# Both MLP halves in block pairs, one block turned on TensorE, and the order from a list scheduler

## The chip, the cores and the metric

The kernel runs on one core of a Trainium2 chip. The metric is the device time of one execution in microseconds. TensorE (PE) multiplies into eight banks of accumulators; VectorE (DVE) and ScalarE (ACT) do the element-wise work; GpSimd (POOL) and SyncE (SP) mostly issue DMAs here. Each engine works off its own instructions in the order in which the program emits them, and they wait for one another by semaphores.

## The reference

```python
x = A_x                       # 2048 rows x 640
xn = _layernorm(x, axis=-1)
# Fourier half: real part of a DFT along the hidden axis and along the sequence
a = einsum("bsd,ed->bse", xn, dft_hid_re); b = einsum("bsd,ed->bse", xn, dft_hid_im)
y = einsum("ts,bse->bte", dft_seq_re, a) - einsum("ts,bse->bte", dft_seq_im, b)
# MLP half: 640 -> 1536 -> 640
h = gelu(einsum("bsd,df->bsf", xn, w1) + b1)
return x + y + einsum("bsf,fd->bsd", h, w2) + b2
```

All is in 32-bit floats. The kernel writes each operand as a high half rounded to TensorE's format (ACT, a copy) and a low half, the rest (DVE, a subtraction), and makes one product of 128x128 weights with 512 columns out of three matmuls: high x high, high x low, low x high.

## The kernel before, in words

The MLP half comes first. The 2048 rows are four blocks of 512; the 640 inputs are five chunks of 128, the 1536 hidden columns twelve units `f` of 128, the 640 outputs five chunks. Layer one of a unit costs five products (15 matmuls, `hidden`, L308, the matmul at L320), layer two five more (`output`, L363, whose three matmuls are at L300 to L302 in `product`). Each unit goes through `gelu` (L354): ACT takes the bias and the gelu out of the bank, ACT writes the high half (`high`, L185), DVE the low half (`low`, L188).

Block 0 comes plain: its rows are normalized, turned on TensorE (`transpose_x`, L680, 20 turns of 128x128), split, and multiplied unit by unit while W1 and W2 are loaded and split. Blocks 1 and 2 go together in `pair` (L1039), six steps `k` of two units each. With sums and differences of the blocks' chunks (the forms `ua`, `va`, `vb`, `t1` to `t4`, `oa`, `ob`) and of W1's columns (the pieces A to D, `make_pieces`, L891), four units of layer one (two units, two blocks) take 18 products where four plain ones take 20. A step holds them in seven windows over three banks; copies out of banks and additions of two banks on ACT and DVE join them. The forms of blocks 1 and 2 are made by turning 32x32 tiles on DVE, after the rows went through memory (`put_z`, `make_forms`). The units of block 2 go to memory (`keep`, L930, issued by POOL) and come back later (`load_unit`), since only one block's five layer-two sums fit beside a pair. Block 3 comes plain again, with W1 loaded and split once more; W2 stays on chip in high and low halves. Block 1's, 2's and 0's results take the bias on ACT, are turned on DVE, added to the residual rows and stored (`finish`, `turn_sum`, `store_sums`).

Beside this run preparations for the Fourier half: five chunks of the hidden DFT matrices are loaded, turned, combined and split (`load_w`, `turn_w`, `prep_w`), and the normalized rows are combined into `xab` and `xc` (`build`, L596). The Fourier half follows from `es_rows.close()` on, and takes the larger part of the time. Before all stand 19 warm-up matmuls (L666).

The order of everything around the matmuls in the MLP half is written out by hand: `background`, `late`, `beside_pair`, `between` and `fourier_step` say what is emitted beside which unit or window.

Of the kernel before, what the change touches and what calls it, by code (L numbers as in the profile page):

```python
# [10 lines left out]
F32 = mybir.dt.float32  # L11
# [4 lines left out]
P = 128  # L16
# [10 lines left out]
def kernel(  # L27
# [71 lines left out]
    gs = dram.tile([NF, P, TB], F32, name="gs")  # L99
# [16 lines left out]
    def bank(k):  # L116
# [3 lines left out]
    pool("pad", side="right").tile([P, 120], F32, name="padr")  # L120
# [4 lines left out]
    MV = const.tile([P, 4, 6], F32, name="mv")  # L125
# [14 lines left out]
    PLACES = [  # L140
# [9 lines left out]
    ]  # L150
    slots = {}
# [5 lines left out]
    def open_place(tag, size, keys):  # L157
        t = place(tag, (P, size // 4))
        for k, key in enumerate(keys):
            slots[key] = t[:, k * 2 * D : (k + 1) * 2 * D].rearrange("p (a b) -> p a b", a=2)  # L160
# [30 lines left out]
    def weave(*lists):  # L191

        for row in zip_longest(*lists):
            for f in row:
                if f:
                    f()
# [5 lines left out]
    xt, slot = {}, {}  # L202

    def load_x(c, eng=nc.sync, k=None, home=None):

        slot[c] = c % NC if k is None else k
        xt[c] = (row_places if home is None else home)[:, slot[c]]
        eng.dma_start(xt[c], x[c * P : (c + 1) * P])

    def ln_stats(c):  # L210
        m = MV
        st = ST[c % 2]
        half = D // 2
        for h in range(2):
            nc.vector.bn_stats(st[:, h, :], xt[c][:, h * half : (h + 1) * half])
        nc.vector.bn_aggr(m[:, slot[c], 0:2], st.rearrange("p a b -> p (a b)"))

    def ln_scale(n):

        m = MV[:, :n]  # L220
        ve, r, t = m[:, :, 2], m[:, :, 3], m[:, :, 4]
# [3 lines left out]
        nc.vector.scalar_tensor_tensor(t, r, -0.5, r, op0=ALU.mult, op1=ALU.mult)  # L225
        nc.vector.tensor_tensor(t, t, ve, op=ALU.mult)
        nc.vector.scalar_tensor_tensor(r, t, 1.5, r, op0=ALU.add, op1=ALU.mult)

    def ln_apply(c, eng=nc.vector):
        m = MV[:, slot[c]]  # L230
        eng.tensor_scalar(xt[c], xt[c], m[:, 0:1], m[:, 3:4], op0=ALU.subtract, op1=ALU.mult)

    def ln_apply_chunked(dst, c, j0=0, j1=ND):

        m = MV[:, slot[c]]
# [8 lines left out]


    XT, zt = {}, {}
    Z = {}

    def new_xt(t):
        w = mr.tile([P, ND, 2, TB], F32R, tag="xt", bufs=1, name=f"xt{t}")  # L250
        for j in range(ND):
            XT[j] = w[:, j]
# [4 lines left out]
    def transpose_z(key, z, j):  # L257
        zt[key] = mr.tile([P, TB], F32, tag="zt", bufs=2, name=f"zt{key}")
        nc.vector.transpose(zt[key].rearrange("p (n i) -> p n i", i=B), z[:, :, j * B : (j + 1) * B])

    def prep_xt(key, j):
        split(XT[j][:, 0], XT[j][:, 1], zt.pop(key))

    W1, W2, w1r, w2r = {}, {}, {}, {}


    AGAIN = (0, 1, 2, 3, 8, 9, 10, 11, 6, 7, 4, 5)

    def load_w1(i, eng=nc.sync):

        if i >= 3 * NF:
            return
        f0 = (i % NF if i < 2 * NF else AGAIN[i - 2 * NF]) * P
        t = early.tile([P, ND, P], F32, tag="w2r" if i == NF + 5 else "w1r", bufs=3, name=f"w1r{i}")
        w1r[i] = t
        v = w1.rearrange("(q c i) f -> q i c f", q=Q, i=B)
        for q in range(Q):
            eng.dma_start(t[q * B : (q + 1) * B], v[q, :, :, f0 : f0 + P])

    def load_w2(i, eng=nc.sync):  # L280
        if i >= NF:
            return
        t = early.tile([P, D], F32, tag="w2r", bufs=3, name=f"w2r{i}")
        w2r[i] = t
        eng.dma_start(t, w2[i * P : (i + 1) * P, :])

    def prep_w1(i, n=None):
        if i < NF:
            W1[i] = slots[1, i]
            split(W1[i][:, 0], W1[i][:, 1], w1r.pop(i if n is None else n).rearrange("p a b -> p (a b)"))  # L290

    def prep_w2(i):
        if i < NF:
            W2[i] = slots[2, i]
            split(W2[i][:, 0], W2[i][:, 1], w2r.pop(i), perm=True)
# [7 lines left out]


    NG = NT * NF
    HT, oacc, xo = {}, {}, {}

    def hidden(g, part=slice(None)):  # L308
        i = g % NF
        acc = bank((5 if g < NF else 0) + g % 3)  # L310
        kinds = ((0, 0), (0, 1), (1, 0))
        steps = [(j, k) for j in range(ND) for k in range(3)]
        if g == 0:
            steps = FIRST
        if g == 1:

            steps.sort(key=lambda s: s[1] == 2)
        for n, (j, k) in list(enumerate(steps))[part]:
            a, b = kinds[k]
            nc.tensor.matmul(  # L320
                acc, W1[i][:, a, j * P : (j + 1) * P], XT[j][:, b], start=n == 0, stop=n == len(steps) - 1
            )
        return acc

    def term(g, acc, a=None):

        if a is None:
            a = mr.tile([P, TB], F32, tag="ab", bufs=2, name=f"ab{g}")
        nc.scalar.activation(a, acc, AF.Copy)
        return a  # L330

    def unit(g, acc, plus=None, a=None):

        i = g % NF
        if a is None:
            a = mr.tile([P, TB], F32, tag="ab", bufs=2, name=f"ab{g}")
        if plus is not None:
            add(a, plus, acc)
            acc = a
        nc.scalar.activation(a, acc, AF.Gelu_apprx_tanh, bias=b1c[:, i : i + 1])  # L340
        return a

    def split_unit(g, a, fill=lambda k: None):
        hs = mr.tile([P, 2, TB], F32R, tag="hs", bufs=3, name=f"hs{g}")
        HT[g] = hs
        high(hs[:, 0], a)
        fill(1)
        low(hs[:, 1], a, hs[:, 0])


    FIRST = [(0, 0), (0, 2), (1, 0), (1, 2), (0, 1), (2, 0), (2, 2), (1, 1), (3, 0), (3, 2)]
    FIRST += [(2, 1), (4, 0), (4, 2), (3, 1), (4, 1)]

    def gelu(g, acc, fill=lambda k: None):  # L354

        a = unit(g, acc)
        fill(0)
        split_unit(g, a, fill)


    OBANKS = ((0, 1, 2, 3, 4), (0, 1, 2, 3, 4), (5, 6, 7, 3, 4), (3, 4, 5, 6, 7))

    def output(g, es=range(ND)):  # L363
# [308 lines left out]

    for p in PLACES[:7]:
        open_place(*p)
# [1109 lines left out]
```

## Time and profile before

| | us |
|---|---|
| median of two runs (850.91 and 851.31) | 851.11 |
| span of the profiled execution | 848.5 |
| its MLP half, to the first matmul of the Fourier half | 329.8 |
| TensorE busy | 842.5 |
| DVE busy | 687.1 |
| ACT busy | 368.8 |

A row of the groups by line reads: line, engine, operation, what is written and read, shapes, count, then busy time, mean nanoseconds of one, and the engine's idle time before them with what ended it. Matmuls overlap, so the mean of one is longer than their spacing. A row of the chain of waits reads: start, duration, what ran. The windows give each engine's busy time within a stretch.

### The profile page before, as it was taken

Reading aid. Unit: us, or ns where it says so; the run is one execution under the profiler, and the core shown is the slowest. Engines: PE = TensorE matmul, PEld = TensorE weight load, DVE = VectorE, ACT = ScalarE, POOL = GpSimd, SP = SyncE. Lnnn points to the kernel's source line nnn. Section 1 sums busy time; section 2 is a strip of 40 time slices with the busy share of each in tenths; the row PEclk is TensorE's granted clock in tenths of the full one; section 3 lists DMA queues with packets and bytes.
Section 4 is the critical chain, followed back from the end, with each engine's and each line's share of the span. In section 5 each row is a group of like instructions: output and inputs, shape, how many; then the busy total and the mean of one; then the engine's idle time right before and its main releaser. Section 6 shows DMA issues by size and latency. Waiting matters only on the chain.

```text
span 848.5 us, 10660 instructions
## 1 busy us (share of the span) xinstructions
PE 842.5 (99%) x3741; PEld 698.6 (82%) x3741; DVE 687.1 (81%) x912; ACT 368.8 (43%) x527; POOL 67.6 (8%) x116
## 2 busy tenths in 40 slices
PE   9999999999999999999999999999999999999998
PEld 7888888888888888888888888888888888888887
DVE  7969888767854778979979787899977998886687
ACT  7655666545453555443444343232322433223241
POOL 0440024222301000000000000000000000000002
PEclk9999999999999999999999999999999999999999
DMA  7995757878987897948744679663744799805354
GB/s 222 291 247 163 149 159 249 265 222 298 254 203 201 336 321 139 208 118 198 156 137 107 167 219 292 158 142 95 218 151 156 230 234 230 311 19 180 124 168 112
DMA packets 197094, 166.53 MB, mean 196 GB/s; under 512 B 59601, under 2 KB 168145, under 8 KB 196529
## 3 DMA queue, kind: packets, MB, share of 16 engines
q1 hardware_dynamic: 187296, 140.42, 61.8%
q0 software_dynamic: 7600, 24.91, 8.8%
q10 hardware_dynamic: 2144, 0.52, 0.3%
q8 instruction: 29, 0.48, 0.2%
q14 instruction: 25, 0.20, 0.1%
HBM read 115.75 MB, written 46.14 MB: 191 GB/s over the span
## 4 chain that ended last, share of the span: by engine, by line
PE 99%; DVE 0%; issue 0%
PE banks L301 30%; PE banks L300 30%; PE banks L302 30%; PE banks L320 10%; PE banks L666 1%; PE banks L682 0%; DVE zeros L655 0%; DVE yo L1706 0%; DVE warm L657 0%
## 5 line engine op out<-in xcount | busy, mean ns | idle before, releaser
L301 PE MATMUL banks<-as,xab 128*128 128x512 f32 (+1 forms) x417 | 160.1, 384 | 0.0
L300 PE MATMUL banks<-as,xab 128*128 128x512 f32 (+1 forms) x417 | 160.1, 384 | 0.0
L302 PE MATMUL banks<-as,xab 128*128 128x512 f32 (+1 forms) x417 | 160.1, 384 | 0.0
L186 ACT ACTIVATE as<-r 128x1024 fp32r<-128x1024 f32 x80 | 85.0, 1062 | 171.2 <-PE banks L302 147.4
L189 DVE TENSOR_TENSOR as<-r,as 128x1024 fp32r<-128x1024 f32 x80 | 97.1, 1215 | 38.1 <-ACT as L186 38.0
L301 PEld LDWEIGHTS banks<-as,xab 128*128 128x128 f32 x417 | 78.3, 188 | 15.6
L300 PEld LDWEIGHTS banks<-as,xab 128*128 128x128 f32 x417 | 78.3, 188 | 15.5
L302 PEld LDWEIGHTS banks<-as,xab 128*128 128x128 f32 x417 | 78.3, 188 | 15.4
L301 PE MATMUL banks<-as,xc 128*128 128x512 f32 x224 | 87.1, 389 | 0.0
L300 PE MATMUL banks<-as,xc 128*128 128x512 f32 x224 | 87.1, 389 | 0.0
L302 PE MATMUL banks<-as,xc 128*128 128x512 f32 x224 | 87.1, 389 | 0.0
L186 ACT ACTIVATE as<-rt 128x1024 fp32r<-128x1024 f32 x32 | 34.0, 1062 | 72.5 <-PE banks L302 57.9
L320 PE MATMUL banks<-xt,xab 128*128 128x512 f32 x240 | 56.8, 390 | 0.0
L189 DVE TENSOR_TENSOR hs<-ab,hs 128x512 fp32r<-128x512 f32 x36 | 24.7, 685 | 36.2 <-ACT hs L186 36.2
L320 PEld LDWEIGHTS banks<-xt,xab 128*128 128x128 f32 x240 | 45.0, 188 | 9.4
L301 PEld LDWEIGHTS banks<-as,xc 128*128 128x128 f32 x224 | 42.0, 188 | 8.8
L302 PEld LDWEIGHTS banks<-as,xc 128*128 128x128 f32 x224 | 42.0, 188 | 8.7
L300 PEld LDWEIGHTS banks<-as,xc 128*128 128x128 f32 x224 | 42.0, 188 | 8.7
L1280 POOL DMA_DIRECT2D out_dram<-u x4 | 2.6, 657 | 568.3 <-DVE u L463 568.3
L300 PE MATMUL banks<-hs,xc 128*128 128x512 f32 x120 | 46.7, 389 | 0.0
L301 PE MATMUL banks<-hs,xc 128*128 128x512 f32 x120 | 46.7, 389 | 0.0
L302 PE MATMUL banks<-hs,xc 128*128 128x512 f32 x120 | 46.7, 389 | 0.0
(240 smaller groups left out, 1679.8 us busy)
## 6 DMA issues: line engine op xcount, KB each, us to landing
raw<-in_A_dft_seq_re_dram SPq DMA_DIRECT2D x64, 256.0 KB, 5.4
raw<-in_A_dft_seq_im_dram SPq DMA_DIRECT2D x64, 256.0 KB, 5.1
w1r<-in_B_w_dram SPq DMA_DIRECT2D x144, 80.0 KB, 3.3
wit<-wst POOLq DMA_DIRECT2D x15, 384.0 KB, 4.3
wit<-wst POOLq DMA_DIRECT2D x20, 256.0 KB, 4.2
forms_ab<-xab SPq DMA_DIRECT2D x4, 1280.0 KB, 7.6
xab<-wit SPq DMA_DIRECT2D x13, 384.0 KB, 4.1
row<-xn SPq DMA_DIRECT2D x14, 320.0 KB, 5.3
```

Source lines behind the costliest of these rows:

```text
L186: nc.scalar.activation(h, s, AF.Copy)
L189: nc.vector.tensor_tensor(l, s, h.bitcast(F32), op=ALU.subtract)
L300: nc.tensor.matmul(acc, wh, mh, start=first, stop=False, skip_group_check=goes_on)
L301: nc.tensor.matmul(acc, wh, ml, start=False, stop=False, skip_group_check=goes_on)
L302: nc.tensor.matmul(acc, wl, mh, start=False, stop=last, skip_group_check=goes_on)
L320: nc.tensor.matmul(acc, W1[i][:, a, j * P : (j + 1) * P], XT[j][:, b], start=n == 0, stop=n == len(steps) - 1)
L666: nc.tensor.matmul(wacc, warm[:, :P], warm, start=True, stop=True)
L1280: queues[q % len(queues)].dma_start(rows_of(out, t)[:, rows, q * DQ + c0 : q * DQ + c1], src[q * B : (q + 1) * B])
```

## The change

The MLP half is written anew; the Fourier half keeps its code, but for two places that exchange names.

- Layer one: blocks 0 and 1 are one pair, blocks 2 and 3 another, each with six steps of 18 products (seven windows of two or three products). Plain blocks are gone.
- Pair 0 begins with block 0 alone: for each even unit, the two windows that need no form of block 1 are run first (`first_unit`, `a_units`, `a_rest`), the unit goes on to layer two, and the sum of the first window is kept on chip (`U[k]`). The other 13 products follow in `rest_of_pair`, after ACT has written `U[k]` back to a bank. In pair 1 the sum goes from one bank to another instead.
- Block 1 is normalized and turned on TensorE like block 0, into banks 0 to 4; its forms are made from there. Blocks 2 and 3 are normalized, written to memory, read back and turned on DVE.
- W1's columns are loaded once for block 0's first windows (the even units) and once for each pair. W2 is split once and stays, in other places than before, in the order 0, 2, ..., 10, 1, 3, ..., 11.
- The units of blocks 1, 2 and 3 all go to memory (`gs` grows to four blocks) and come back for layer two, which runs for block 0 beside pair 0 and for the others one after another.
- Normalizing of blocks 1 to 3 uses ACT for most rows.
- Two of the five chunks of the hidden matrices are prepared after the forms of pair 0 (`w_early`), three after those of pair 1 (`w_late`).
- The order of emission comes from a list scheduler that runs while the program is built: each piece of work is a generator that yields an engine, an assumed duration, a function and its needs; `work` keeps an assumed clock for each engine and always emits the step with the least start time plus weight. 93 weights stand in the source.

The diff, cut to its core:

```diff
-    gs = dram.tile([NF, P, TB], F32, name="gs")
+    gs = dram.tile([NT, NF, P, TB], F32, name="gs")
...
+    LAG = {"pe": 0.3, "act": 0.12, "dve": 0.12}
...
+    def pe(n, fn, *needs, w=None):
+        return op("pe", n * 0.68, fn, needs, w)
+    def act(n, fn, *needs, w=None, table=None):
+        return op("act", 0.1 + n * 0.00094, fn, needs, w) + (table,)
+    def dve(n, fn, *needs, w=None):
+        return op("dve", 0.08 + n * 0.00108, fn, needs, w)
...
+    def work(goal=None):
+        while threads and (goal is None or goal not in done):
...
+                start = max(t, clock[want[0]])
+                score = start + (th[2] if want[4] is None else want[4])
+                if best is None or score < best[0]:
+                    best = score, start, th
...
+    def a_units():
+        mark(("va", 0), 14.9)
+        for k in range(1, 6):
+            n, t = yield BANK
+            t = yield pe(2, lambda: window(bank(n), f"Au{k % 2}", 0, "ua", True), ("A", k), t)
+            spawn(a_rest(k, n, t), W("a_rest", 0.0))
...
+    def a_rest(k, n, t):
+        acc = bank(n)
+        t = yield act(TB, lambda: copy(U[k], acc), t, w=W("op1", -0.3))
+        mark(("U", k), t)
+        t = yield pe(3, lambda: window(acc, f"Av{k % 2}", 0, "va", False, (f"Av{k % 2}", 2, "oa0")), t)
...
+    def next_rows():
...
+            t = yield pe(0.7, lambda: [turn_row(c, j) for c in range(NC)], *needs)
+            mark(("T", j), t)
...
+    def rest_of_pair(p, k, nx, nz, t):
...
+        tx = yield pe(2, lambda: window(x_, c, 0, "t2", False), (p, "x", k), (p, "C", k), ("X", p, "t20"), ("X", p, "t21"))
...
+        tv = yield act(TB, lambda: copy(v, x_), tx, tv, w=W(f"op3{p}", -0.3))
+        tz = yield pe(3, lambda: window(z_, d, 2, "t1", True, (b, 2, "ob0")),
+                      t, (p, "D", k), (p, "B", k), ("X", p, "t10"), ("X", p, "t11"), ("X", p, "ob0"))
...
+        tc = yield act(TB, lambda: copy(zc, z_), tz, tc, w=W(f"op2{p}", -0.3))
+        tx = yield pe(2, lambda: window(x_, d, 0, "t3", False), tv, ("X", p, "t30"), ("X", p, "t31"))
...
+        spawn(z_and_b(p, k, z_, nz, tc, v, tv), W(f"z_and_b{p}", -0.01))
+        ta = yield dve(TB, lambda: add(zc, zc, x_), tx, tc, w=W(f"op4{p}", -0.3))
...
+        tx = yield pe(3, lambda: window(x_, b, 0, "t4", False, (b, 2, "oa0")), ta, ("X", p, "t40"), ("X", p, "t41"))
...
+    def first_pair():
+        yield ("X", 0, "t10")
+        for k in range(NF // 2):
+            nx, t = yield BANK
+            t = yield act(TB, lambda: copy(bank(nx), U[k]), t, ("U", k))
...
+            spawn(rest_of_pair(0, k, nx, nz, t), W(f"rest0{k // 5}", 0.001))
+            yield (0, "t3", k)
...
+    def second_pair():
...
+            t = yield pe(2, lambda: window(bank(ny), f"Bu{k % 2}", 0, "ua", True), t, (1, "Au", k))
...
+            t = yield act(TB, lambda: copy(bank(nx), bank(ny)), t, tx, w=W("op5", -0.3))
+            mark((1, "x", k), t)
+            spawn(other_unit(k, ny, t), W(f"other{k // 5}", 0.002))
...
+            spawn(rest_of_pair(1, k, nx, nz, tz), W(f"rest1{k // 5}", 0.001))
...
+    def rows_again():
...
+        for token in (("rest", 0), (0, "z1", 5), *((0, "x", k) for k in range(2, 6))):
+            yield token
+        Z[2] = region("wa", "z2", F32).rearrange("p (n d) -> p n d", d=DQ)
+        t = yield dma(6.1, lambda: load_z(Z[2], 2), ("xn", 2), n=4)
```

More of the change, by code (lines that the diff above doesn't have):

```diff
@@ L302, in product @@
         nc.tensor.matmul(acc, wl, mh, start=False, stop=last, skip_group_check=goes_on)
[L305 to L323, printed above, removed]
@@ L651 @@
+    yt2 = rows.tile([P, 2, TB], F32, name="yt2")
+    zeros = yt2[:, 0]
+    warms = [early.tile([P, D], F32R, tag=f"raw{k}", bufs=1, name=f"warm{k}")[:, :TB] for k in range(3)]
     for c in range(NC):
@@ new lines, with halves @@
+    first_unit(slice(1, None))
+    clock.update(pe=14.8, act=13.2, dve=13.9, sp=13.5, pool=5.0, dma=14.0)
+    for c in range(NC, 2 * NC):
+        mark(("x", c), 12.0 + 0.5 * (c - NC))
+    RAW = Slots()
+    RAWA = Slots()
+    XT = Slots()
+    TMP = Slots(*(tmp[:, k] for k in range(4)))
+    YT = Slots()
+    HS = Slots(hs2[:, 0], hs2[:, 1])
+    BANK = Slots()
+    U = [yt2[:, 0], yt2[:, 1], wc[:, :TB], wc[:, TB:], tu[:, :TB], tu[:, TB:]]
+    F = {}
+    Z = {}
+    def halves(name, hi, lo, src, *needs, n=TB):
+        t = yield act(n, lambda: high(hi, src), *needs)
+        t = yield dve(n, lambda: low(lo, src, hi), t, *needs)
+        mark(name, t)
+        return t
@@ new lines, in all_builds @@
+    def all_builds():
+        yield ("rest", 1)
+        yield (1, "va", 5)
+        yield "w"
+        A["sums"] = zo_tile("sums", (P, 2, 9 * P))
+        yield from rows_for(0)
+        yield from rows_for(1)
+        for k in range(len(builds) - 1):
+            if k == 6:
+                yield ("xr", 7)
+            yield from build_one(k)
+    F[0] = zo_tile("f0", (P, ND, TB))
+    spawn(a_pieces(), W("a_pieces", 0.0))
+    spawn(first_a(), W("first_a", 0.0))
+    spawn(a_units(), W("a_units", 0.0))
```

1550 lines of the change are left out of this document (945 added, 605 removed), and 9 rows, old and new, of the table PLACES.

## The prediction

> **What bounds the kernel now.** I read the page's head and engine totals first, then the view of waits for TensorE, the chain of waits, the groups by line, and last the windows.
>
> ```profile
> span 848.5 us, 10660 instructions
> PE 842.5 (99%) x3741; PEld 698.6 (82%) x3741; DVE 687.1 (81%) x912; ACT 368.8 (43%) x527; POOL 67.6 (8%) x116
> ```
>
> ```profile
> PE banks L666 <- DVE warm L657: 1.9, 1, 1.9
> ```
>
> ```profile
> 1.92 7.49 PE banks L666 x19
> 9.41 2.08 PE banks L682 x19
> 11.50 0.24 PE banks L320
> 11.85 10.03 PE banks L320 x44
> 25.28 3.40 PE banks L320 x15
> ...
> 844.47 0.45 DVE yo L1706
> ```
>
> The second fence is the whole answer on TensorE's waits: one, of 1.9 us, before the first warm-up matmul. The third is the chain of waits (start, us, what). From 1.92 us on TensorE never waits, until the last matmuls give way to the stores. So the time is a count of matmuls times their spacing: 15 in 3.40 us, 0.2267 us each. A 128x128 turn on TensorE (L682) took 2.08 / 19 = 0.109 us. The span can shrink only if TensorE gets less to do, and every microsecond for which it waits is added. The profiled execution spans 848.5 us against a median of 851.11; the 2.6 us around it I add back at the end.
>
> **What the change takes from TensorE and gives to it.**
>
> ```profile
> L320 PE MATMUL banks<-xt,xab 128*128 128x512 f32 x240 | 56.8, 390 | 0.0
> L320 PE MATMUL banks<-xt,as 128*128 128x512 f32 x120 | 28.5, 389 | 0.0
> L300 PE MATMUL banks<-xab,w1f 128*128 128x512 f32 x72 | 28.0, 389 | 0.0
> L300 PE MATMUL banks<-as,w1f 128*128 128x512 f32 x36 | 14.0, 389 | 0.0
> L682 PE MATMUL banks<-ident,xp 128*128 128x128 f32 x20 | 2.5, 273 | 0.0
> ```
>
> Layer one before: blocks 0 and 3 plain, 2 x 12 columns x 15 matmuls = 360, the two L320 rows. Blocks 1 and 2 as pairs: 72 + 36 = 108 products of three matmuls (L300 to L302), 324. Together 684. After: both pairs have six steps of 18 products. In pair 0, first_unit and a_units make 5 of the 18, rest_of_pair 13; in pair 1 second_pair makes 2, other_unit 3, rest_of_pair 13. That is 2 x 6 x 18 x 3 = 648. **36 matmuls go: 36 x 0.2267 = 8.2 us.** Layer two stays at 4 x 12 x 5 products, and the Fourier half is untouched. **20 turns come: 20 x 0.109 = 2.2 us.** Net 6.0 us less, if TensorE still never waits: 842.5 span. That is the floor.
>
> By the Trainium skill ("TensorE: Matmul & The Clock Gate", Part 4) a turn takes about 275 ns in a kernel. Its 20 would be 5.5 us; the spacing here says 2.2, and only the length of one (273 ns, overlapped with its neighbours) agrees.
>
> **What it adds on the other engines, and whether TensorE must wait for them.**
>
> ```profile
> L189 DVE TENSOR_TENSOR hs<-ab,hs 128x512 fp32r<-128x512 f32 x36 | 24.7, 685 | 36.2 <-ACT hs L186 36.2
> L189 DVE TENSOR_TENSOR xab<-w1r,xab 128x640 fp32r<-128x640 f32 x15 | 12.2, 817 | 0.8 <-ACT xab L186 0.8
> L189 DVE TENSOR_TENSOR w1f<-w1r,w1f 128x384 fp32r<-128x384 f32 x6 | 3.3, 551 | 0.6 <-ACT w1f L186 0.6
> L463 DVE TENSOR_TENSOR w1r<-w1r,w1r 128x256 f32<-128x256 f32 x12 | 5.1, 425 | 0.4
> L463 DVE TENSOR_TENSOR w1r<-w1r,w1r 128x128 f32<-128x128 f32 x6 | 1.7, 284 | 0.0
> L259 DVE STREAM_TRANSPOSE ztx<-z 128x512 f32<-128x512 f32 x5 | 3.4, 699 | 0.0
> L215 DVE BATCH_NORM_STATS2 st<-row 128x6 f32<-128x320 f32 x14 | 6.1, 476 | 1.5 <-DMA row<-in_A_x_dram 1.5
> L216 DVE BATCH_NORM_AGGREGATE mv<-st 128x2 f32<-128x12 f32 x15 | 3.1, 209 | 0.5
> L403 DVE STREAM_TRANSPOSE row<-row 128x640 f32<-128x640 f32 x10 | 7.9, 825 | 0.7 <-DMA row<-in_A_dft_hid_im_dram 0.7
> L329 ACT ACTIVATE ab<-banks 128x512 f32<-128x512 f32 x7 | 4.1, 583 | 0.7 <-PE banks L302 0.7
> L186 ACT ACTIVATE xab<-w1r 128x640 fp32r<-128x640 f32 x15 | 10.9, 734 | 6.1 <-DMA w1r<-in_B_w_dram 6.1
> L714 ACT ACTIVATE xp<-row,mv 128x640 f32<-128x640 f32 x1 | 0.9, 909 | 0.0
> L186 ACT ACTIVATE hs<-ab 128x512 fp32r<-128x512 f32 x36 | 22.8, 632 | 1.1
> ```
>
> ```profile
> 15.00:169.00 154.00, 154.00 (x681) 127.52 (x680) 129.71 (x251) 95.66 (x169) 39.18 (x67) 1.00 0.80 221
> 169.00:330.00 161.00, 161.00 (x712) 133.29 (x712) 110.89 (x224) 83.30 (x154) 22.57 (x34) 1.00 0.83 249
> ```
>
> The windows' columns are the stretch, its length, then TensorE, weight loads, DVE, ACT, POOL, the clock, the DMA share and GB/s. TensorE is full in both; DVE had 154.0 - 129.7 = 24.3 us free in the first.
>
> ACT: the one pair of before had three 512-wide copies a step (first sum, v, zc), 18. Pair 0 now has four (the first sum is kept in U and written back to a bank), pair 1 three: 42, so 24 more at 0.583 = 14 us. A copy from on-chip memory into a bank is in no row; its nearest are the copy out of a bank (L329, 0.583) and the one beside the banks (L186, 0.632), and I take 0.6. Most of the normalizing of blocks 1 to 3 goes to ACT too, 12 steps of the 0.909 of L714, 11 us. ACT had 154.0 - 95.7 = 58 us free in the first stretch, which hides both; without that cover the 25 us would show.
>
> DVE is the tight one. Up to the first matmul of pair 1 TensorE has 15 x 5 matmuls for the other units of block 0 (17.0 us), 20 turns (2.2), layer two of blocks 0 and 1 (360 matmuls, 81.6), and rest_of_pair six times (39 matmuls, 53.0): 153.8 us. DVE must finish beside that, at the means above:
> - statistics of blocks 1 to 3, 12 x (2 x 0.476 + 0.209) = 13.9, and some 7 for scales and the normalizing left on it: 21
> - low halves of W1 for five units, 5 x 0.817 = 4.1; of W2, as wide, 12 x 0.817 = 9.8
> - low halves of 24 units 16.4; 13 sums of two banks 8.9
> - forms of pair 0: 8 sums, 11 low halves, 13.0; its pieces, 6 x (0.551 + 0.817 + 0.685 + 4 x 0.425 + 0.284) = 24.2
> - two of the five chunks of the hidden matrices (w_early), each two turns (0.825), four sums of 0.425, one of 0.284, seven low halves of about 0.42 and four of 0.284, 7.7: 15.4
> - sums of block 0: 5 x (0.699 + 0.685) = 6.9
> - forms of pair 1: 10 turns, 8 sums, 16 low halves, 23.4; its first pieces 5.0.
>
> Total 148 of 153.8 us. These means overlap when one step follows another; five low halves in a row go faster:
>
> ```profile
> 11.36 3.07 DVE L189 TENSOR_TENSOR xt<-banks,xt 128x512 fp32r<-128x512 f32 x5
> 13.55 1.81 SPq L278 DMA_DIRECT2D w1r<-in_B_w_dram  x4
> ...
> w1r<-in_B_w_dram SPq DMA_DIRECT2D x144, 80.0 KB, 3.3
> xo<-in_A_x_dram SPq DMA_DIRECT2D x12, 320.0 KB, 6.4
> xab<-in_A_x_dram SPq DMA_DIRECT2D x4, 320.0 KB, 10.2
> ```
>
> 3.07 / 5 = 0.614 against 0.685, a factor 0.90: 133 us. DVE is 87 to 96% full where it was 84%. It fits, but each place where TensorE needs a piece at a set time counts:
> - **Third unit of block 0.** Its W1 columns go into the tile that the first unit's columns leave. That low half ends at 11.36 + 3.07 + 0.82 = 15.25; four issues 1.81, landing 3.3, high half 0.73, low half 0.82: 21.9. TensorE ends the first unit at 11.85 + 14 x 0.2267 = 15.0, and two units later wants it at 21.8, its low half 0.45 later. Free if DVE is idle then; one step in front costs 0.7. I take 0.7.
> - **Banks 0 to 4.** The turned block 1 sits in them until its forms are made; layer two of block 0 needs them. DVE: first low half to 15.25, statistics 4 x 1.16, a sum and a low half 1.5, six small steps for the scale, each like L216's 0.209, two normalizations 1.8: 24.5. The turns go behind the third unit, 25.2 to 27.4. Six DVE steps and two ACT steps later, with units and W1 in between, the banks are free at 32 to 36; units four and five keep TensorE until 34.2. I take 0.5. Behind a waiting turn stand all later matmuls; who waits is every unit.
> - **Into pair 1.** The rows of blocks 2 and 3 are read back (load_z) once pair 0 has left its places: SP waits there, and behind it stand W1's next columns, the unit loads and the residual rows. Rows like these took 6.4 to 10.2 us. Layer two of block 1 covers 40.8 us, in which DVE still owes some 33. I take 0.3. If the cover were gone the whole 10 us would show.
> - POOL writes 36 units to memory, not 12 (L931); SP reads them back. Nothing on TensorE waits for POOL unless it is several microseconds late. 0.
>
> Bounds of this idle time: 0 to 4 us (each place doubled and a little for steps of the pairs), nothing below 0. I take 1.5, nearer to 0 because the old order, with DVE at 84%, lost nothing. **Sum: 848.5 - 8.2 + 2.2 + 1.5 = 844.0 span, 846.6 us by the median.**
>
> **The rivals.**
> - *DVE sets the pace to pair 1.* The trace speaks for it: 24.3 us of waiting sat in DVE's queue in the first stretch. If that stays, DVE needs 133 + 24.3 = 157 or 148 + 24.3 = 172 us for 153.8, so TensorE idles 3.5 to 18.5 us. Against: much of that waiting was slack, not need. With 8, since busy stretches run at the spacing, 848.5 - 6.0 + 8 = 850.5, so 853.1.
> - *Slower: the hops inside a pair step.* A step's chain is copy into the bank, t2, copy, t3, sum, t4: two copies and a sum on in-order engines between windows that wait for one another. For: behind DVE at 90% each hop can stand behind a 0.8 us step. Against: the pairs of before have like hops in three banks and no wait. Three hops x 0.8 = 2.4 us in each of 12 steps is 29 us: 848.5 - 6.0 + 29 = 871.5, so 874. It is slower by 2% from (17.0 + 6.0) / 12 = 1.9 us per step.
> - *One long gap and a slow restart.* 19 warm-up matmuls took 7.49 us, 0.394 each; after a long gap 19 at that rate would cost 19 x (0.394 - 0.227) = 3.2 us on top. A gap of 4 us, say at the banks, gives 848.5 - 6.0 + 1.5 + 7.2 = 851.2, so 853.8. The Trainium skill ("TensorE: Matmul & The Clock Gate", Why this matters for your kernels) has such a rule: one idle window of about 3 us halves the clock. The slow first row fits that; the trace has no gap to test it.
> - *The saving is eaten by the turns.* If a turn between matmuls cannot overlap and costs its whole 0.273 us (L682's mean of one), 20 cost 5.5: 848.5 - 8.2 + 5.5 + 1.5 = 847.3, so 849.9. The 19 in a row speak against it.
>
> **How the numbers follow.** Forecast 0.60 (845.1 to 849), DVE 0.20 (848.6 to 863.6), hops 0.08, restart 0.06, turns 0.06. The range takes the first, the last two and the lower half of DVE's: 845.0 to 855.5, some 0.82. A change of 2%, 17 us, is about what a measurement of this kernel can tell from none. The floor is 0.7% below before, so faster has 0.01; slower is the hops' 0.08, as DVE's far end stays under 868; the rest, 0.91, is within.
>
> **What would show it.** TensorE with 3725 matmuls, of them 648 in layer one and 40 turns; TensorE busy near 836.5. Its waits: under 2 us together, first around 22 and 34 us. DVE's rival shows as TensorE waiting for the L189-like low halves between 100 and 170 us; the hops as a dozen equal waits in the pair steps; the restart as 0.39 us between matmuls after a gap. I am wrong if TensorE idles over 4 us, or if the count differs.

## The result, and the profile after

The changed kernel took 922.68 us (922.14 to 923.23, 2 runs) against 851.11 before, a ratio of 1.0843 (1.0811 to 1.0874): 72 us slower. The prediction had said 846.6, in a range up to 855.5. The profiled execution spans 921.5 us. The page's head, its engine totals, and the clock row in 40 slices:

```profile
span 921.5 us, 10713 instructions
PE 862.5 (94%) x3725; PEld 703.3 (76%) x3725; DVE 699.0 (76%) x955; ACT 394.4 (43%) x581; POOL 80.8 (9%) x131
PEclk9999997989999998999999999999999999999999
```

TensorE issues 3725 matmuls and turns, 16 fewer than before, and yet the span is longer. The view of TensorE's waits had one line before; now it begins so (what waited, for what: us in total, times, longest):

```profile
PE banks L329 <- ACT hs L180: 22.3, 10, 10.1
PE banks L330 <- DVE hs L183: 16.3, 13, 4.2
PE banks L1110 <- ACT rt L246: 5.0, 2, 4.1
PE banks L329 <- DVE tmp L189: 4.4, 2, 3.1
PE banks L329 <- ACT yt L186: 2.4, 1, 2.4
```

`hs` are a hidden unit's high and low halves: most of the waiting is layer two's first product of a unit waiting for that unit. The windows (columns as above) show where; the first fence is the changed kernel, the second the kernel before:

```profile
0.00:100.00 100.00, 84.57 (x348) 66.92 (x348) 72.76 (x162) 70.58 (x119) 16.06 (x33) 0.95 0.66 185
100.00:200.00 100.00, 73.27 (x269) 56.61 (x270) 47.24 (x99) 40.37 (x72) 15.73 (x26) 0.85 0.65 181
200.00:300.00 100.00, 97.80 (x428) 79.80 (x427) 82.27 (x166) 62.29 (x126) 35.78 (x54) 1.00 0.76 221
402.00:921.00 519.00, 514.72 (x2298) 426.92 (x2296) 436.12 (x410) 179.62 (x186) 5.19 (x8) 1.00 0.66 173
```

```profile
0.00:100.00 100.00, 98.08 (x430) 81.13 (x431) 83.52 (x161) 62.56 (x99) 18.30 (x39) 1.00 0.82 217
100.00:200.00 100.00, 100.00 (x443) 82.81 (x442) 77.22 (x167) 58.01 (x123) 30.06 (x51) 1.00 0.75 226
330.00:848.00 518.00, 514.44 (x2298) 426.99 (x2296) 434.63 (x407) 179.30 (x186) 5.16 (x8) 1.00 0.65 173
```

The Fourier half takes 519 us here and 518 there, with the same 2298 matmuls. All of the loss is in the MLP half, most of it before 200 us: up to 100 us TensorE starts 348 matmuls instead of 430, from 100 to 200 us 269 instead of 443, and there every other engine is *less* busy than before: DVE 47 us of 100, ACT 40, POOL 16, DMA 0.65. No engine is full there; they wait for one another.

From the starts of all matmuls the loss can be split. I took each distance to the next start, less what that matmul needs (0.2267 us, a turn 0.109); what lies in stretches with a granted clock of one half I counted apart, and a rest of over 0.3 us as a wait. Before: 0.4 us of waits and 2.7 of small rests. After: **60.4 us in 36 waits, 14.9 us lost at half clock, 6.4 of small rests**. That is 78.6 us more, less the 6.0 us of work that went: 72.6, and the spans differ by 73.0.

The largest wait, in the chain of waits and in the timelines of ACT and TensorE (start, us, what):

```profile
137.57 1.39 POOL xn L253 x3
139.22 8.46 DMA xn<-r
147.79 0.74 ACT r L180
...
153.82 0.61 DVE hs L183
154.48 0.79 PE banks L330
```

```profile
147.79 0.74 ACT L180 ACTIVATE r<-raw 128x640 fp32r<-128x640 f32 x1 [10.01 <-DMA xn<-r]
...
150.69 0.61 ACT L180 ACTIVATE hs<-tmp 128x512 fp32r<-128x512 f32 x1
```

```profile
151.36 0.80 PE L329 MATMUL banks<-hs,r 128*128 128x512 f32 x1 [10.14 <-ACT hs L180]
154.48 0.79 PE L330 MATMUL banks<-hs,r 128*128 128x512 f32 x1 [2.33 <-DVE hs L183]
155.07 0.63 PE L331 MATMUL banks<-hs,r 128*128 128x512 f32 x1
155.50 0.63 PE L329 MATMUL banks<-hs,r 128*128 128x512 f32 x1
```

Read it from the back (`r` here is the place of W2's last units and, before that, of block 3's rows). TensorE waits for a high half; the high half stands in ACT's queue behind the split of one of W2's last three units (`r<-raw`); that split stands 10.01 us until its place is free, which is when block 3's normalized rows, which lie there, have been stored (`xn<-r`). W2's unit was in no hurry; what stood behind it was. After the gap the matmuls come 0.43 us apart instead of 0.2267.

### The profile page after: what moved, and what is told of

Its sections match the earlier page's. It is cut to its first block, busy times and chain, and to the rows that moved or that the text cites. A ratio compares the mean times of both kernels' runs of the same rounds, so it can differ in the third digit from the quotient of the medians.

```text
span 921.5 us, 10713 instructions
## 1 busy us (share of the span) xinstructions
PE 862.5 (94%) x3725; PEld 703.3 (76%) x3725; DVE 699.0 (76%) x955; ACT 394.4 (43%) x581; POOL 80.8 (9%) x131
## 4 chain that ended last, share of the span: by engine, by line
PE 72%; DMA 8%; DVE 7%; issue 6%; ACT 3%; SPq 3%; POOL 1%; DVEq 0%; ACTq 0%; POOLq 0%
PE banks L330 24%; PE banks L331 24%; PE banks L329 24%; DMA forms_c<-xc 3%; DMA xn<-r 2%; DMA pairs<-in_B_w_dram 1%; DMA wit<-wst 1%; DVE hs L183 1%; SPq L1410 1%; SPq L386 1%; DVE as L183 1%; DVE r L451 1%; DMA raw<-in_B_w_dram 1%; SPq L306 1%; DMA row<-in_A_x_dram 0%
## 5 line engine op out<-in xcount | busy, mean ns | idle before, releaser
L180 ACT ACTIVATE as<-rt 128x1024 fp32r<-128x1024 f32 x80 | 85.0, 1062 | 168.6 <-PE banks L331 147.2
L183 DVE TENSOR_TENSOR as<-rt,as 128x1024 fp32r<-128x1024 f32 x80 | 97.1, 1215 | 37.9 <-ACT as L180 37.7
L180 ACT ACTIVATE as<-r 128x1024 fp32r<-128x1024 f32 x32 | 34.0, 1062 | 72.4 <-PE banks L331 57.9
L183 DVE TENSOR_TENSOR hs<-tmp,hs 128x512 fp32r<-128x512 f32 x44 | 29.8, 687 | 36.0 <-ACT hs L180 35.9
L180 ACT ACTIVATE hs<-tmp 128x512 fp32r<-128x512 f32 x44 | 27.3, 628 | 48.3 <-PE banks L331 45.1
L183 DVE TENSOR_TENSOR as<-r,as 128x1024 fp32r<-128x1024 f32 x32 | 38.8, 1212 | 6.5 <-ACT as L180 6.5
L180 ACT ACTIVATE as<-u 128x1024 fp32r<-128x1024 f32 (+1 forms) x24 | 22.1, 919 | 48.1 <-PE banks L331 48.1
L451 DVE STREAM_TRANSPOSE rt<-raw 128x1024 f32<-128x1024 f32 x32 | 39.6, 1241 | 2.6 <-PE banks L331 2.0
L183 DVE TENSOR_TENSOR as<-u,as 128x1024 fp32r<-128x1024 f32 (+1 forms) x24 | 24.9, 1042 | 18.8 <-ACT as L180 18.8
```

Source lines behind the costliest of these rows:

```text
L180: nc.scalar.activation(h, s, AF.Copy)
L183: nc.vector.tensor_tensor(l, s, h.bitcast(F32), op=ALU.subtract)
L451: nc.vector.transpose(held(pieces[g][2], u).rearrange("p c (n i) -> p c n i", i=B), r.rearrange("p n (c i) -> p c n i", i=B))
```

## How the order came about

The order on each engine is fixed when the kernel is built. The scheduler in the source lets the operation with the smallest planned start plus weight go next, by a clock of its own. How its 93 weights were chosen, no run here shows; that this plan has so little idle time (below) suggests that they were chosen by that clock. An operation counts as ready when all times in its list of needs have passed. But in several places the source waits for a token and does not pass on its time:

```
            t = yield ("H", t_, f_)
            hs = done["hs", t_, f_]
            t = yield pe(len(es), lambda: output(t_, f_, hs, es), ("W2", f_), *extra)
...
                yield ("xn", 3)
                open_place("r01")
```

The first `t`, the time at which a hidden unit's halves are ready, is overwritten before it is used. The second is the place of W2's last units: the plan lets the split go as soon as block 3's store has been *issued*. On the chip both waits are real.

I matched the scheduler's operations one by one with the trace's instructions, in order of issue on each engine. By the plan TensorE's MLP work ends at 330.5 us with 6.5 us idle; in the trace it ends at 401.9, and its last operation starts **71.3 us behind plan**, about as much as the whole loss. (The plan itself promised nothing over the kernel before, whose MLP half ends near 329: 848.5 less the 519.6 us from 401.9 to the end here.) The store above was planned to be issued at 112.0 and to land at 119.3; it was issued at 137.6, and what waited for it went on at 147.8.

I came to this only after a first theory had fallen, so the runs are told in their order. Two rivals were kept throughout: VectorE has too much to do, and the single place for W1's columns (or the contention of transfers) holds everything up.

## The experiments

The kernel before ran beside each group, at 850.5 to 851.4 us. The runs e1 to e12 are single ones. Four runs of e13 lie 5.5 us apart, so a difference of some 6 us or less between two single runs shows nothing by its size.

**First theory: transfers land later than planned.** One edit in the scheduler:

```diff
-                    end = clock["dma"] + 2.0
+                    end = clock["dma"] + 5.0
```

> All work is done and the products are the same; only the list scheduler's assumed time from a DMA's turn to its landing goes from 2.0 to 5.0 us, so the order in which each engine's instructions stand may change. Theory (in-order queues stand on transfers that land later than the scheduler assumed, 60 us of TensorE waits and 15 us of half clock behind them): TensorE's waits fall by a third or more, span 865 to 900. Rival 'one buffer' (W1's columns have one place, and each of its loads lies on the path whatever the order): no gain, 915 to 935. Rival 'VectorE' (it has too much to do in the new half): no gain, 915 to 930.

Measured: 945.33 us, span 943.6, with 79.1 us of waits. The theory expected a span of 865 to 900 and fell; the rivals' bands, which end at 930 and 935, were missed too. By that clock 76.8 us of idle time were planned, and the chip delivered what was planned.

Three runs moved transfers and buffers, with the scheduler's clock left as it was.

```diff
-    EARLY_W = 2
+    EARLY_W = 0
```

> The hidden matrices' first two of five chunks, whose transfers and GpSimd stores ran beside blocks 0 and 1, are prepared with the other three, behind the first pair's layer one; the rest of the program is the same and all work is done. Theory: the second load of W1's columns (landed 12.1 us after its issue) and the stores of the normalized rows (landed 5 to 8 us after) have the queues to themselves in the first pair; the gaps between 60 and 130 us shrink from 12.5 us to under 6, the 10.1 + 2.3 us at 151 stay: span 900 to 915. Rival 'contention is all of it': 870 to 885, also the gap at 151 goes. Rival 'VectorE': no gain, since the same work falls into the later stretch, 920 to 930. Rival 'one buffer': 915 to 922.

Measured: 925.24 us, span 923.5, 62.2 us of waits. No gain; the expected 900 to 915 was missed, and the number lies in the band of the VectorE rival. The gaps did what the theory said where it had looked: TensorE's idle time from 60 to 130 us fell from 13.1 to 5.6 us, and the largest wait stayed (at 135 instead of 151, 11.87 us). But from 320 us on it rose from 10.0 to 23.6 us.

```diff
+        zo = zo_tile("pairs_b", (P, NB * DQ))
+        PAIRS.put(zo[:, : ND * 2 * P].rearrange("p (a b) -> p a b", b=2 * P), 0.0)
```

> As e2_all_late, and the room that this leaves holds a second place for W1's columns during the first pair, so that a step's load no longer waits for the turn of the step before it; all work is done. Theory: gaps in the first pair that end at a rounding copy which waited for such a load (5.78 and 5.26 us of ScalarE waits, at 61 and 106 us) go, those at 151 to 158 and 187 to 194 stay: 5 to 15 us below e2_all_late, 885 to 910. Rival 'one buffer' (it is the whole cause): below 880. Rival 'VectorE': as e2_all_late within 3 us.

Measured: 930.97 us, span 929.2, against 885 to 910 expected, and 5.7 us above e2: a second place for W1's columns brought no gain. The largest wait, 10.64 us at 128, is in another place of TensorE's order, but the same split stands before it in ACT's queue (ACT's timeline of this run):

```profile
126.51 0.74 ACT L180 ACTIVATE r<-raw 128x640 fp32r<-128x640 f32 x1 [7.84 <-DMA xn<-r]
```

```diff
-                yield ("xn", 3)
+                yield ("xn", 1)
...
-        src = rows_in("r01")
+        src = row_places
```

> As e4_two_w1, and blocks 2 and 3's rows go to another place, so that the rounding of W2's last three units no longer waits until block 3's normalized rows are stored (ScalarE waited 10.01 us for that store at 147.8 us); the load of the hidden matrices' first chunk waits for it instead. All work is done. Theory: the gap of 10.1 + 2.3 us and the half clock behind it (144.3 to 158.0, some 3 us lost) go: 12 to 16 us below e4_two_w1, 870 to 897. Rival 'it is hidden' (something else ends there just as late): within 4 us of e4_two_w1. Rival 'VectorE': within 4 us of e4_two_w1.

Measured: 919.72 us, span 918.0, 11.3 below e4, a little less than the 12 to 16 expected; the span itself was expected at 870 to 897, as e4's had been expected lower. (By the edit, what waits for block 3's store instead is the load of block 0's residual rows.) No wait of over 4 us is left between 30 and 325 us. But those at 326 to 364 us (3.19, 5.50, 5.79) stay; e2 and e4, which share the edit of `EARLY_W`, have them too (7.02 and 5.08, 7.65 and 5.32), and the changed kernel has none of over 3.3 us there, so they came with that edit. So this one is only 3 us below the changed kernel: one wait can be taken out, and what the edits before it had brought is still there.

**Second theory: the plan leaves waits out.** First only the bookkeeping was mended: the time of each hidden unit, of W2's and the rows' places and of the reloads goes into the needs. Weights, instructions and real waits stay.

```diff
-            t = yield pe(len(es), lambda: output(t_, f_, hs, es), ("W2", f_), *extra)
+            t = yield pe(len(es), lambda: output(t_, f_, hs, es), t, ("W2", f_), *extra)
...
-                yield ("xn", 3)
+                home = yield ("xn", 3)
                 open_place("r01")
...
-        t = yield act(D, lambda: high(chunked(hi), s), t)
+        t = yield act(D, lambda: high(chunked(hi), s), t, home)
```

> All work is done; nothing but the list scheduler's own bookkeeping changes: the time at which a hidden value's halves are ready goes into the needs of layer two's products, and the time at which a place or a row buffer comes free goes into the needs of what is put there (W2's split behind block 3's stored rows, blocks 2 and 3's rows, the z read-back, the hidden matrices' loads). The program's real waits are the same as before, its weights too; the order may differ. By its own clock this order leaves TensorE idle for 51 us, where the changed kernel's left 6.5 and the chip showed 52.7. Theory (the planned order is poor because the plan's clock leaves these waits out): the chip now agrees with the plan, idle 45 to 70 us, span 905 to 935, no gain, since weights chosen by the wrong clock stay. Rival 'landing times' (transfers land later than planned, whatever the plan knows of waits): idle well over its plan, 75 us or more, span over 935.

Measured: 919.54 us, span 917.8; TensorE idle 47.4 us as the trace counts it. Time as before, as expected; but now the plan says so. TensorE's end was planned at 375.0 and measured at 398.9: 23.8 us behind plan where it had been 71.3. With nothing but the waits made known, two thirds of the error of the plan are gone, and the chip's time is the same. (That plan and chip agree is not proof enough: e1, by its slow clock, is no further behind plan. The searches below are the test.)

Then the weights were chosen anew for this clock, by trying random changes and keeping the better:

> As e6_waits_known, and the scheduler's weights (which say how far a thread's work is put back) are chosen anew for that clock; by it TensorE is idle for 13.3 us in the MLP half. The work, the buffers and the products are the same. Theory 'order' (the loss is in the order, which was chosen by a clock that left waits out): idle 18 to 38 us, span 860 to 892. Rival 'design' (one place for W1's columns, one shared place for W2 and the rows: the loss is there whatever the order): idle 45 us or more, span 905 or more. Rival 'contention of transfers': idle 40 us or more, with gaps that end at rounding copies behind W1's loads.

Measured: 924.19 us, span 922.4, against 860 to 892 expected; by its total this run lies with the rival "design". The windows and the waits say why:

```profile
0.00:349.00 349.00, 331.32 (x1427) 267.20 (x1427) 226.94 (x464) 189.69 (x344) 73.42 (x122) 0.99 0.72 204
349.00:389.00 40.00, 1.10 (x4) 0.50 (x2) 28.01 (x59) 15.16 (x32) 2.04 (x2) 0.56 1.05 342
```

```profile
PE banks L329 <- ACT xab L1556: 43.3, 3, 38.9
```

The MLP half ended at 349.2 us, 53 us earlier than in the changed kernel and 10.9 behind plan. But I had chosen the weights for TensorE's end alone, and they put off the preparation of the Fourier half's operands (`xab`): DVE had 36 us less done by then, and TensorE stood 38.9 us for it.

In the next the clock's costs also come from the changed kernel's trace:

```diff
-        return op("dve", 0.08 + n * 0.00108, fn, needs, w)
+        return op("dve", 0.135 + n * 0.00108, fn, needs, w)
...
-                    clock[engine] = start + th[1][5] * (0.46 if engine == "sp" else 0.65)
+                    each = 0.46 if engine == "sp" else 0.65
+                    if engine == "sp" and th[1][5] == 8:
+                        each = 1.0
+                    clock[engine] = start + th[1][5] * each
```

> As e7_waits_search, and the clock's costs are taken from the trace of the changed kernel: 0.055 us more for each VectorE operation, at least 0.5 us for a ScalarE one, 1.0 us of issue for each of the eight transfers that load a chunk of the hidden matrices, 1.5 us more for the normalized rows' store. By that clock TensorE is idle for 23.4 us. Theory 'order': the chip comes nearer to the plan than in e7_waits_search, idle 20 to 34 us, span 860 to 885. Rivals as there: 905 or more. If it is slower than e7_waits_search, the added costs are not what that plan missed.

Measured: 929.83 us, span 928.1, with the same fault (one wait of 48.5 us). The span was expected at 860 to 885; that it came out slower than e7 was to speak against the added costs, but the wait after the MLP half hides what they did. In the MLP half the plan was good: TensorE's end planned at 349.7, measured at 355.8, only 6.0 us behind. So of the 71.3 us some 47 went with the waits made known (71.3 to 23.8). What the costs add cannot be told: e7 without them is 10.9 behind, and the later orders by the clock of e6 and e7 are 24 behind (table below).

With the preparation in the aim, and e6's clock (against e6 only the weights' numbers differ):

> As e7_waits_search, whose weights had been chosen for the end of TensorE's work in the MLP half alone (its preparation of the Fourier half's operands fell behind, and TensorE then stood 38.9 us at 388); here they are chosen for the later of TensorE's end and the end of that preparation plus 14 us. All work is done, with the same instructions and buffers. By its clock TensorE's MLP work ends at 344.9 us and is idle for 20.9 us on the way. Theory 'order' (the plan's clock left waits out, and the order was chosen by it): the MLP half ends between 355 and 368 us where the changed kernel's ended at 401.9, no gap of over 6 us after it, span 872 to 890. Rival 'design' (VectorE, or the places, cannot do the work in less whatever the order): span 905 or more, since what e7 gained in the MLP half must come back in the preparation.

Measured: 891.74 us, span 890.0, 31 us less than the changed kernel with the same instructions and buffers. The upper end of 890 was just met; the MLP half ended at 369.3, a little over the 355 to 368.

**Is it the transfers after all?** Two runs keep the changed kernel's order to the last instruction and make transfers small; they leave out part of the data, so their results are not the reference's. In the first, W1's step loads of the first pair:

```diff
-                t = yield dma(1.85, lambda: w1_rows(r, 2 * k, 2), t, n=4)
+                t = yield dma(1.85, lambda: w1_rows(r, 2 * k, 2, rows=ND if p else 1), t, n=4)
```

> The changed kernel with the order of its instructions kept; the six step loads of W1's columns in the first pair move one row group of five instead of all (the other columns of the place stay what they were, so these products are not the reference's). Nothing else differs. Theory 'order' (the order was planned by a clock that left waits out): only the waits that end behind such a load go, 5.8 and 5.3 us of ScalarE's and what of them reached TensorE: span 905 to 919. Rival 'one place for W1's columns, landing late' (it is the cause of most of the 60 us): span below 890.

Measured: 914.15 us, span 912.4. With a fifth of the bytes in these loads 9 us go; 54.2 us of waits stay. ACT's and TensorE's timelines have the same waits, 9.4 us earlier:

```profile
138.40 0.74 ACT L180 ACTIVATE r<-raw 128x640 fp32r<-128x640 f32 x1 [9.90 <-DMA xn<-r]
```

```profile
141.96 0.80 PE L329 MATMUL banks<-hs,r 128*128 128x512 f32 x1 [10.03 <-ACT hs L180]
145.09 0.79 PE L330 MATMUL banks<-hs,r 128*128 128x512 f32 x1 [2.33 <-DVE hs L183]
```

In the second the early loads of the hidden matrices as well:

```diff
+            n = 2 if j < EARLY_W else ND * Q
-            nc.sync.dma_start(t[q * B : (q + 1) * B], v[:, :, s0 : s0 + B])
+            nc.sync.dma_start(t[q * B : (q + 1) * B, :n], v[:, :n, s0 : s0 + B])
```

> As e10_small_w1, and the early two chunks' loads of the hidden matrices move two of twenty column groups each (the prepared forms of these chunks are then not the reference's), so that little moves on SyncE's queue beside the first pair. The order of the instructions is still the changed kernel's. Theory 'order': TensorE's waits stay at 40 us or more, span 895 to 915. Rival 'contention of transfers': waits below 25 us, span below 885.

Measured: 920.53 us, span 918.8, 57.5 us of waits, even more than e10; the expected 895 to 915 was too low, the rival's 885 far off. The waits of 10.00 and 2.33 us stand as they were. So it is not contention with these loads that makes them; block 3's store itself was not made smaller in any run. Why e11 is 6 us above e10 is open; single runs can lie that far apart.

**Would any new weights have helped?** The control is a search in the same manner and for the same aim by the old clock, with the waits left out:

> A control for the searches of e7 and e9: weights searched anew in the same manner and for the same aim as e9's, but by the changed kernel's own clock, with the waits left out. By that clock TensorE's MLP work ends at 338.9 us with 14.8 us idle, 6 us earlier than e9's did by its clock. All work is done. Theory 'order planned by a clock that leaves waits out': the chip does not follow this plan, the MLP half ends at 375 us or later and the span is 895 to 935. Rival 'any new weights help' (the first ones were an unlucky draw, the clock is good enough): the MLP half ends before 362 us, span below 885.

Measured: 923.86 us, span 922.1. Planned end 338.9, measured 403.3, 64.3 us behind. By its own clock this plan was 6 us better than e9's; on the chip it was 32 us worse. New weights as such do not help, then. It is one search by the old clock, but all four searches by a clock that knows the waits (e7, e8, e9, e13) end the MLP half at 349 to 369 us, and by the old clock the changed kernel and this one end it at 402 and 403.

**The best order**, e9's search continued:

> As e9_search_all, searched on from its weights: by the clock that knows the waits TensorE's MLP work ends at 342.0 us with 18.0 us idle, the preparation at 327.4 (e9: 344.9, 20.9 and 332.2; the chip took 24 us longer than the plan there). All work is done. Theory 'order': 2 to 6 us below e9, span 882 to 890, time 884 to 892, still 4% above the kernel before, since the plan's own idle time and the costs that the clock still has too low are left. Rival 'the searches had reached what the chip follows': within 2 us of e9 or above it.

Measured: 885.9 us (882.75 to 888.24, 4 runs), as expected, a ratio of 1.0405 to the kernel before (1.0376 to 1.0435). The windows of this kernel and of the changed one up to the end of the MLP half:

```profile
0.00:366.00 366.00, 337.63 (x1428) 271.23 (x1429) 263.23 (x547) 217.26 (x397) 75.11 (x123) 0.97 0.80 236
```

```profile
0.00:402.00 402.00, 347.81 (x1429) 276.39 (x1430) 262.85 (x546) 214.77 (x396) 75.60 (x123) 0.94 0.72 214
```

DVE does the same 263 us of work in 366 us that it had in 402. VectorE's work is not what made it 402, then. Nor is "one place for W1's columns" the cause of the whole: that place is still single here. ACT's wait for block 3's store is not gone, but is 1.9 us where it was 10.0 (ACT's view of waits, this kernel):

```profile
ACT r L180 <- DMA xn<-r: 1.9, 1, 1.9
```

The plans and the chip together (planned and measured end of TensorE's MLP work; behind plan by the start of its last operation; the last three columns are of the whole kernel, from the starts of matmuls):

| kernel | planned end | measured end | behind plan | waits | lost at half clock | span |
|---|---|---|---|---|---|---|
| before | - | near 329 | - | 0.4 | 0 | 848.5 |
| after | 330.5 | 401.9 | 71.3 | 60.4 | 14.9 | 921.5 |
| e1 landing 5 us | 400.8 | 424.8 | 23.8 | 79.1 | 16.5 | 943.6 |
| e6 waits known | 375.0 | 398.9 | 23.8 | 54.8 | 14.1 | 917.8 |
| e7 and search | 338.1 | 349.2 | 10.9 | 67.1 | 9.4 | 922.4 |
| e8 and costs | 349.7 | 355.8 | 6.0 | 72.7 | 8.2 | 928.1 |
| e9 aim mended | 344.9 | 369.3 | 24.3 | 35.6 | 7.7 | 890.0 |
| e12 old clock | 338.9 | 403.3 | 64.3 | 55.7 | 20.4 | 922.1 |
| e13 searched on | 342.0 | 366.1 | 23.9 | 30.2 | 9.5 | 884.9 |

In e7 and e8 the waits include the one behind the MLP half. e1's clock lets every transfer land later, which hides the waits that it leaves out: the run keeps nearer to its plan, and the plan is bad.

So an order searched by a clock that knows the waits, with the preparation in the aim, gives back 37 us of the 72. What is left, 35 us, is again waits (30.2 us) and half clock (9.5), and its cause is not settled. Of e13's own plan 18.0 us are idle, and the plan ends 13 us after the kernel before; the other 24 lie between plan and chip. The largest waits of its first 30 us behind the warm-up (1.77 and 4.32 us) are for a copy out of a bank and for block 1's normalized rows, which the old kernel did not need so early. Whether a longer search, more places or another design would win these back was not tried beyond the runs above; no order found here comes near the kernel before.

## Why the prediction was wrong

**The count was right.** 3725 matmuls and turns stand on the page, as worked out; the Fourier half did not change. The floor of 842.5 us was a floor and nothing more. "TensorE busy near 836.5" was not met (862.5): matmuls at half clock count longer, and so do those behind a wait (0.80 us at 151.36 above).

**The step that failed is the idle time:** "Bounds of this idle time: 0 to 4 us [...]. I take 1.5, nearer to 0 because the old order, with DVE at 84%, lost nothing." It was 60.4 us of waits, and 14.9 at half clock, for which the sum had no term. The old order was written by hand around TensorE; the new one came out of a scheduler, and no row of the old trace could speak for it. I added up busy time and asked whether the work fits. It does: from 15 us to the first product of pair 1 at 185.7 us DVE was busy 101 us, less than the 133 to 148 of my list (part of it, much of pair 1's forms, came later in this order). But whether the work comes in time hangs on what stands ahead of it in each queue. The source says that, in its lists of needs, and I had not read them against the waits of the program.

- *Third unit of block 0*, taken at 0.7: TensorE did not wait for its columns (their low half was done at 20.52 us, TensorE came to them at 21.56). But their split had waited 1.80 us at the head of ACT's queue, and behind it stood a copy out of a bank for which TensorE stood 2.35 us in the middle of the second unit (first two lines below). No term of mine had that copy.
- *Banks 0 to 4*, taken at 0.5: the turns waited 4.15 and 0.89 us for block 1's rows, and the clock fell to half behind them. DVE's chain was priced; what stood ahead in ACT's queue was not: a split, a gelu and two table loads, from 20.85 on (ACT's timeline):

```profile
17.11 0.74 ACT L180 ACTIVATE wa<-raw 128x640 fp32r<-128x640 f32 x1 [1.80 <-PE banks L331]
18.70 1.09 ACT L186 ACTIVATE yt<-banks 128x512 f32<-128x512 f32 x2
...
20.85 0.74 ACT L180 ACTIVATE as<-raw 128x640 fp32r<-128x640 f32 x1 [0.43 <-DMA raw<-in_B_w_dram]
21.61 1.28 ACT L343 ACT_TABLE_LOAD   x1
22.91 0.69 ACT L343 ACTIVATE tmp<-banks,b1c 128x512 f32<-128x512 f32 x1
23.61 1.28 ACT L216 ACT_TABLE_LOAD   x1
24.91 0.30 ACT L216 ACTIVATE padr<-padr,eps 128x4 f32<-128x4 f32 x1
26.26 0.92 ACT L246 ACTIVATE rt<-r,padr 128x640 f32<-128x640 f32 x1 [1.05 <-DVE padr L222]
```

- *Into pair 1*, taken at 0.3: 3.73 and 0.61 us at 192 to 194, behind the forms of pair 1, whose last rows had landed at 183.1 (and 1.44 us at 173, just before).
- *POOL*, "Nothing on TensorE waits for POOL unless it is several microseconds late. 0.": it was late, and nothing had been put down for that. The largest wait of all, 10.14 and then 2.33 us, hangs on a store that POOL issued at 137.6, planned for 112.0. ACT's free time (58 us of 154) was no cover: the wait at its queue's head took the cover away for everything behind it.

**The rivals.** *DVE sets the pace* was wrong, though its sign, waits for low halves between 100 and 170 us, did appear (4.17 us at 127, 2.33 at 154). DVE was busy 47 us of 100 there. Before both it had stood behind ACT, 5.24 us up to 107 and 10.09 up to 148.6, and then worked off what had piled up (DVE's timeline):

```profile
148.56 0.83 DVE L183 TENSOR_TENSOR r<-raw,r 128x640 fp32r<-128x640 f32 x1 [10.09 <-ACT r L180]
```

*Hops in the pair steps* was nearest in size (874) and mostly wrong in place: 38.6 us of the waits stand at layer two's products (the rows with `hs`), 4.4 at a window that waits for a sum of two banks (L189). *One long gap and a slow restart* had the mechanism and not the number: nine slow stretches in the MLP half, not one, and far more waiting than its 4 us. *The turns* cannot be told apart from the waits around them. That the order itself could be bad, because its planner leaves waits out, was no rival of mine, and it should have been the first.

## What to carry to other kernels

When a change hands the order to a scheduler, compare its list of needs with the program's real waits before pricing anything: a wait that the plan does not know is planned at zero, and an in-order engine makes everything behind it pay. Match planned starts with the trace, operation by operation; the time behind plan says whether the chip can follow the plan, though not whether the plan is good (e1). And a search is as good as its clock and its aim: one by the wrong clock gained nothing here, two with the wrong aim moved the wait elsewhere.

## What the runs showed of the hardware

A short wait can be followed by half clock. In the changed kernel 1.44 us and then 0.23 us were enough, with no other idle time since 154.5 us (TensorE's timeline; matmul starts go from 0.23 to 0.43 us apart at 175.04 and back at 178.42, so for 3.4 us; the record of the granted clock shows one half there):

```profile
173.28 0.49 PE L329 MATMUL banks<-hs,r 128*128 128x512 f32 x1 [1.44 <-ACT hs L180]
174.00 0.50 PE L330 MATMUL banks<-hs,r 128*128 128x512 f32 x1 [0.23 <-DVE hs L183]
...
174.81 0.40 PE L330 MATMUL banks<-hs,r 128*128 128x512 f32 x1
175.04 0.59 PE L331 MATMUL banks<-hs,r 128*128 128x512 f32 x1
175.43 0.63 PE L329 MATMUL banks<-hs,r 128*128 128x512 f32 x1
...
178.42 0.43 PE L330 MATMUL banks<-hs,r 128*128 128x512 f32 x1
178.69 0.39 PE L331 MATMUL banks<-hs,r 128*128 128x512 f32 x1
```

A wait of 2.35 us at 19.4 us, on the other hand, was followed by matmuls at full speed. The Trainium skill ("TensorE: Matmul & The Clock Gate", Part 1) has a free-running window of about 3.4 us over which activity is watched, and a clock that is either full or half; the length of the stretch and the spacing agree. The advice of the Trainium skill to avoid gaps of over about 3 us ("TensorE: Matmul & The Clock Gate", Why this matters for your kernels) is too generous for this trace: 1.7 us, in two gaps, were enough once.

The issue of transfers took longer than planned: eight loads of a chunk of the hidden matrices kept SP for 9.2 us, from 54.79 to 63.99, where the plan had 3.7, and W2's next unit stood behind them (SP's timeline):

```profile
54.79 5.89 SPq L386 DMA_DIRECT2D row<-in_A_dft_hid_re_dram  x4
60.74 3.25 SPq L386 DMA_DIRECT2D row<-in_A_dft_hid_im_dram  x4
64.49 0.82 SPq L1040 DMA_DIRECT2D raw<-in_B_w_dram  x2
```
